# A transformer block on one core: the second norm's transposes behind every second group of pairs, and other turns for ScalarE's sums

## The chip, the cores and the metric

The kernel runs on one core of a Trainium2 chip. The metric is device time in microseconds (us); each figure is the median of several executions. Five engines work side by side, each in the order of its own instruction stream: TensorE (PE in the profile, with its weight loads as PEld), VectorE (DVE), ScalarE (ACT), GpSimd (POOL) and SyncE (SP, which only issues transfers here). They wait for each other by semaphores. TensorE writes its results into eight banks of PSUM, each 128 partitions by 512 fp32 columns; VectorE and ScalarE read them out.

## The reference

A block with an adaptive layer norm, full attention over 32 heads of 16 columns and a gated feed-forward network (FFN), for one sequence of 2048 rows and 512 columns. All is fp32, and the tolerance is such that the kernel splits operands into a high and a low part and adds three products.

```python
mod = (_silu(c) @ w_mod).reshape(c.shape[0], 6, 1, -1)
sa, ca, ga, sb, cb, gb = (mod[:, k] for k in range(6))
h = _layernorm(x) * (1 + ca) + sa
x = x + ga * attention(h, wqkv, wo)      # softmax(q k^T / 4) v, 32 heads of 16, then @ wo
h = _layernorm(x) * (1 + cb) + sb        # the second norm
x = x + gb * ((_silu(h @ w_gate) * (h @ w_up)) @ w_down)
```

## The kernel before, in words

**Units, steps and pairs.** After the projections, attention is done in 32 *units* (`NU`): four chunks of 512 query rows, and in each eight groups of four heads. A unit has 16 *steps*, one for each 128 keys, and a step has four *pairs* (`pair_of`, L977), one for each head. A pair is two matmuls, which lie in different halves of TensorE's rows and run together: the score of one head for 128 keys and 512 queries (`score`, L569), which ScalarE turns into exponentials (L571), and a score block of a unit some 20 steps ahead (`max_one`, L521), of which VectorE takes only the row maxima (L523). So each pair costs VectorE one reduction of 128x512 and ScalarE one exponential of 128x512. The variable `done` counts pairs; the first 12 come before the schedule below. There are 2048 in all, that is 512 steps.

**The second matmul.** `pv_step(i, half)` (L584) multiplies the exponentials of step `i` with V for half of the queries. It is four matmuls in four column groups of TensorE, and it adds into bank 7 over the 16 steps of a unit. There is only this one bank for it (`single`). Behind the last half of a unit ScalarE copies the bank out (L588), and `close_unit` (L924) starts what follows: transfers, a reciprocal, a product on GpSimd, and the loads for a unit three further on. `pvs` (L1012) issues the halves: never a step `i` with `4*i + 8 > done`, because its exponentials would be too fresh. In a plain group it stops behind a closed unit (`break`, L1024) and keeps what it owes for the next group; in a filler block it does not stop.

**Two kinds of stretch.** `plain(steps)` (L1041) is attention alone, in *groups* of three pairs, each followed by one or two PV halves (`HALVES` = 2, 1, 1, 2 in turn, and one more in the last group of a call). The maxima take the banks 0, 3, 1, 2 in turn, the scores 4, 5, 6. A list `tails` can put a function behind a group's pairs; it gets the next of the four banks of the maxima. `filled(places, work)` (L1056) is a *block* of eight pairs, with matmuls of a projection or of the FFN between them (`places` says how many behind which pair); they add into the banks 3 and 6, the maxima have 0, 1, 2 and the scores 4, 5. At its end come the evictions (`hook`) and then `pvs(6, False)`.

**The order by hand.** The loop at L1085 goes over the first three chunks. For each: `plain` up to the step in `STARTS` (147, 275, 403); four blocks with the output projection (`out_pair`, two for each two tiles of 128 rows); the second norm in a plain stretch; then the FFN in blocks: for each of 14 tiles of the hidden layer a `gate_up` (two blocks), for each two of them two `down` (one block each), and a `plain(WIN)` of three steps ahead of the last two. For the third chunk a `plain(REST)` stands between the norm and the FFN, and the last seven jobs are left for the end of the kernel. In `done`, chunk 0 has its projection from 588 to 620, the plain stretch from 620 to 668 and the FFN from 668 to 1016; chunk 1 the same 512 pairs later.

**The second norm.** `add_o` (L801) adds the projection to x on VectorE (L808), tile by tile, and orders ScalarE's sums: `minus_mean` (L816) and `squares` (L820), each over 128x512 with the sum of a row as a by-product. The list `behind` holds such functions with a number of *turns*; `turns_behind` counts them down at the end of each group or block and calls what has come to zero. `scaled` (L902) then forms the scale: three small steps on VectorE (L743 to L745), a chain on GpSimd (L752 to L756), four normalizations there (L765); it also orders the first load of FFN weights. `turned` (L768) is the tail: four transposes of 128x128 on TensorE into one bank (L770), ScalarE's eviction with the modulation (L772), and two operations on GpSimd (L773, L774), which leave the high and the low part for the FFN.

**The row maxima of a unit.** When all maxima of a unit are there, `after(i)` (called when `done // 4` has come to `i + 2`) hands them over, for `i + 21` = 15 mod 16. In a plain stretch it is `max_rows` (L525): a negation on ScalarE (L540), and two turns later four small matmuls into the next bank of the scores (L533 to L535), ScalarE's copy (L537) and two transfers (L539) into two rows of that unit's queries. In a filler block it is `max_turned` (L543), which has no matmul: VectorE transposes (L551, L553) and eight transfers carry the rows (L560). `beside` (L948) says which.

Of the kernel before, what the change touches and what calls it, by code (L numbers as in the profile page):

```python
# [26 lines left out]
NK = D // P  # L27
# [12 lines left out]
WIN = 3  # L40
# [3 lines left out]
PTS = 13  # L44
FBANKS = (3, 6)
KEEP = 7
REST = 24
NORM = 9
STARTS = (147, 275, 403)
TWO = (0, 3, 2, 2, 2, 2, 1, 0)  # L50
DOWN = (0, 3, 3, 0, 3, 3, 0, 0)
# [50 lines left out]
def block_kernel(ctx, tc, x, wqkv, wo, w_gate, w_up, w_down, c, w_mod, out):  # L102
# [391 lines left out]
    posts, behind = [], []  # L494
# [134 lines left out]
    def tile_mid():  # L629
        return pf.tile([P, 2, CW], F32R, name="mid", tag="mid", bufs=3)  # L630

    def tmp(name):
        return pf.tile([P, CW], F32, name=name, tag="tmp", bufs=4)
# [167 lines left out]
    def add_o(ch, t0, outs, late):  # L801
        if ch.mv is None:
            ch.mv = pf.tile([P, 4, 2], F32, name="mv2", tag="mv2", bufs=1)
            ch.rs = pf.tile([P, 4], F32, name="rs", tag="rs", bufs=1)
            ch.rs2 = pf.tile([P, 2, 4], F32, name="rs2", tag="rs2", bufs=1)
        for e in range(2):
            t = t0 + e
            nc.vector.tensor_add(ch.x2[:, t, :], outs[e], ch.x2[:, t, :])  # L808

        def sums(t):  # L810
            st = pf.tile([P, 6], F32, name="stt", tag="stt", bufs=2)
            nc.vector.bn_stats(st, ch.x2[:, t, :])
            nc.vector.bn_aggr(ch.mv[:, t, :], st)

        def minus_mean(t):
            nc.scalar.activation(tmp("sq"), ch.x2[:, t, :], AF.Identity, scale=-1.0 / D,  # L816
                                 accum_out=ch.mv[:, t, 0:1])

        def squares(t):
            nc.scalar.activation(tmp("sq"), ch.x2[:, t, :], AF.Square, bias=ch.mv[:, t, 0:1],  # L820
                                 accum_out=ch.mv[:, t, 1:2])

        if late:
            turns = (1, 2, 2, 3) if t0 == 0 else (1, 2, 3, 4)
            works = ((minus_mean, t0), (squares, t0), (minus_mean, t0 + 1), (squares, t0 + 1))
            behind.extend([k, lambda f=f, t=t: f(t)] for k, (f, t) in zip(turns, works))
        else:
            for e in range(2):
                sums(t0 + e)

    def out_pair(ch, t0, outs, halves):
        return accumulate(outs, lambda e, a, k: ch.oT[a][:, k, (t0 + e) * P:(t0 + e + 1) * P],
                          lambda b, k: ch.wo[k // 2][:, b, k % 2, :], NK,
                          lambda: posts.append(lambda: add_o(ch, t0, outs, True)), halves)
# [67 lines left out]
    def scaled(ch):  # L902
        ch.load_gu(0)
        ch.norm_scale(nc.gpsimd)
        ch.nt = [tile_mid().bitcast(F32) for _ in range(2)]
        for t in range(4):
            ch.normalize(t)
# [69 lines left out]
    def pair_of():  # L977
        nonlocal done
        i = done // 4 - 1
        most = 4 * n - 4 * (LEAD - 1)  # L980
        h = (ORDER if done < most else (0, 1, 2, 3))[done % 4]
        work = [lambda: score(i + 1, h)]
        if done < most:
            work.insert(1 - h % 2, lambda: max_one(done + 4 * (LEAD - 1)))
        for f in work:
            f()
        done += 1
        if side:
            side.pop(0)()
# [22 lines left out]
    def pvs(most, by_halves):  # L1012

        nonlocal owed
        if by_halves:
            most, owed = most + owed, 0
        while most and halves and 4 * halves[0][0] + 8 <= done:
            i, half = halves.pop(0)
            pv_step(i, half)
            most -= 1  # L1020
            if i % 16 == 15 and half:
                close_unit(i // 16, done // 4 - 1)
                if by_halves:
                    break  # L1024
        if by_halves and most and halves and 4 * halves[0][0] + 8 <= done:
            owed = most

    def turns_behind():
        for b in list(behind):
            b[0] -= 1  # L1030
            if not b[0]:
                b[1]()
                behind.remove(b)

    def end_steps():
        nonlocal ended
        while ended < done // 4:
            after(ended - 1)
            ended += 1

    def plain(steps, tails=()):  # L1041

        nonlocal four, bank, beside
        beside = False
        assert steps % WIN == 0 and done % 4 == 0
        four, bank = Turn(0, 3, 1, 2), Turn(4, 5, 6)
        for w in range(4 * steps // WIN):
            for _ in range(WIN):
                pair_of()
            if w < len(tails) and tails[w]:  # L1050
                tails[w](four())
            pvs((HALVES[(w - 2) % 4] if done > 8 else 0) + (w == 4 * steps // WIN - 1), True)
            turns_behind()
            end_steps()

    def filled(places, work):  # L1056

        nonlocal four, bank, beside
        beside = True
        four, bank = three, Turn(4, 5)  # L1060
        if done >= 4 * n - 4 * (LEAD - 1):
            places, bank = ALONE.get(places, places), Turn(4, 5, 0, 1, 2)
        for r in range(len(places)):
            pair_of()
            take(work, places[r])
            if r % 4 == 3:
                end_steps()
        hook()
        pvs(6, False)
        turns_behind()  # L1070
# [14 lines left out]
    for ci in range(last):  # L1085
        plain(STARTS[ci] - done // 4)
        ch = chunks[ci]
        for t0 in (0, 2):
            work = out_pair(ch, t0, outs, True)
            filled(TWO, work)  # L1090
            filled(TWO, work)
        behind.append([4, lambda: scaled(ch)])
        tails = [lambda tp, k=k: ch.turned(tp, k) for k in range(NK)]
        plain(NORM, [None] * NORM + tails[:3])
        plain(WIN, tails[3:])
        if ci == last - 1:
            plain(REST)
        for _ in range(len(ch.jobs) - (KEEP if ci == last - 1 else 0)):
            job, args = ch.jobs.pop(0)
            if args == (NF // FG - 1, 0):  # L1100
                plain(WIN)
            work = job(ch, *args, outs, True)
            for places in (TWO, TWO) if job is gate_up else (DOWN,):
                filled(places, work)
# [5 lines left out]
    turns = chain([2, 3, 2, 0, 1, 2, 0], cycle([1, 3, 2, 0]))  # L1110
# [19 lines left out]
    ch, chp = chunks[last], chunks[last - 1]  # L1130
# [10 lines left out]
    for t in range(4):  # L1141
        out_terms(ch, t, banks[t], (NK - 1,))
        if t % 2:
            add_o(ch, t - 1, banks[t - 1:t + 1], False)
# [40 lines left out]
```

## Time and profile before

| | |
|---|---|
| median of 3 runs | 1829.32 us (1829.18 to 1830.04) |
| span of the profiled execution, first to last instruction | 1827.6 us |
| granted TensorE clock, mean | 1.000 |
| TensorE busy | 1818.3 us (99%) |
| VectorE busy | 1523.2 us (83%) |
| ScalarE busy | 1255.7 us (69%) |
| GpSimd busy | 459.9 us (25%) |
| HBM, over the span | 144 GB/s |

The profiled execution has its span alone on record, not a time of its own like the runs; the median of the runs is 1.7 us above the span, for what lies around the first and the last instruction. Matmuls are pipelined and their ends are modelled, so TensorE shows as busy nearly all the time, also where it waits: what a stretch costs is read from the starts of its instructions, and from the gaps of VectorE. In a row of the timeline the first number is the start in us from the start of the span, the second how long the row lasts; `x6` says that six instructions of a kind are merged into it, and a bracket gives the idle time ahead of it and whose end ended it.

### The profile page before, as it was taken

What the parts mean: (1) busy time and instruction counts of PE and PEld (TensorE: products, weight loads), DVE (VectorE), ACT (ScalarE), POOL (GpSimd) and SP (SyncE); (2) the same over time, 40 slices, a digit from 0 to 9 for tenths busy, and PEclk for the clock granted to TensorE, in tenths of its full rate; (3) what the DMA queues carried; (4) which work ended last, traced back from release to release, by engine and by line L of the source; (5) the groups of instructions that cost most, each with busy time, mean ns of one, the idle gap of its engine ahead of it and who ended that gap; (6) DMA issues with size and microseconds to landing.
All of it is one profiled execution on the core that took longest, in us unless ns stands there. A gap on an engine that the chain in (4) does not pass through costs nothing.

```text
span 1827.6 us, 41072 instructions
## 1 busy us (share of the span) xinstructions
PE 1818.3 (99%) x16904; PEld 1199.7 (66%) x16904; DVE 1523.2 (83%) x2554; ACT 1255.7 (69%) x2434; POOL 459.9 (25%) x538
## 2 busy tenths in 40 slices
PE   9999999999999999999999999999999999999999
PEld 7876444444455777776565777776464577767887
DVE  5578999999999888889999888889999988821544
ACT  4223888888888776777888777777888877774211
POOL 3612544556223111111123111111113011130200
PEclk9999999999999999999999999999999999999999
DMA  9884876667845454453544554444643536333742
GB/s 306 288 225 143 202 195 178 178 167 200 206 81 125 103 123 142 114 148 71 144 110 107 139 125 119 124 115 91 160 79 57 119 89 162 130 119 120 276 167 110
DMA packets 80488, 267.63 MB, mean 146 GB/s; under 512 B 19604, under 2 KB 24212, under 8 KB 59620
## 3 DMA queue, kind: packets, MB, share of 16 engines
q1 hardware_dynamic: 61324, 179.71, 34.1%
q0 software_dynamic: 18288, 84.49, 19.4%
q8 instruction: 133, 2.18, 0.5%
q10 hardware_dynamic: 688, 0.80, 0.2%
q14 instruction: 55, 0.45, 0.1%
HBM read 201.85 MB, written 62.13 MB: 144 GB/s over the span
## 4 chain that ended last, share of the span: by engine, by line
PE 82%; DVE 14%; ACT 1%; DMA 1%; issue 0%; SPq 0%; DVEq 0%; ACTq 0%
PE bank L584 21%; PE bank L786 20%; PE bank L569 14%; DVE mx L523 14%; PE bank L521 11%; PE bank L211 7%; PE bank L796 7%; DMA wm_ab<-in_w_mod 1%; PE bank L770 0%; DMA kop<-o_dr 0%; PE bank L163 0%; DMA rb<-d_dr 0%; ACT sq L820 0%; PE bank L839 0%; DVE v_flat L870 0%
## 5 line engine op out<-in xcount | busy, mean ns | idle before, releaser
L523 DVE TENSOR_REDUCE mx<-bank 128x1 f32<-128x512 f32 x2048 | 1274.3, 686 | 108.3 <-PE bank L521 54.6
L569 PE MATMUL bank<-qop,kop 50*128 50x512 f32 x2048 | 728.6, 425 | 0.4 <-ACT pt__16523 L571 0.2
L521 PE MATMUL bank<-kop,qop 48*128 48x512 f32 x2048 | 725.1, 425 | 0.3
L569 PEld LDWEIGHTS bank<-qop,kop 50*128 50x128 f32 x2048 | 343.6, 184 | 167.9 <-issue 49.7
L521 PEld LDWEIGHTS bank<-kop,qop 48*128 48x128 f32 x2048 | 344.0, 185 | 107.0 <-DVE mx L523 62.3
L786 PE MATMUL bank<-act,wgu 64*128 64x512 f32 x1872 | 301.4, 392 | 0.0
L786 PEld LDWEIGHTS bank<-act,wgu 64*128 64x128 f32 x1872 | 197.1, 187 | 24.3
L611 POOL TENSOR_TENSOR on<-o,rb 128x512 f32<-128x512 f32 x31 | 39.8, 1285 | 506.3 <-DMA rb<-d_dr 358.9
L786 PE MATMUL bank<-wd,mid 64*128 64x512 f32 x912 | 134.1, 397 | 0.1
L858 POOL CAST mid<-m 128x512 fp32r<-128x512 f32 x40 | 24.3, 607 | 380.9 <-DVE m L856 180.2
L786 PEld LDWEIGHTS bank<-wd,mid 64*128 64x128 f32 x912 | 88.3, 186 | 15.5 <-ACT first L893 3.2
L211 PE MATMUL bank<-hT,wqs 128*128 128x512 f32 x384 | 94.4, 397 | 0.4 <-DVE wqs L351 0.4
L854 DVE SCALAR_TENSOR_TENSOR q<-th,bank 128x512 f32<-128x512 f32 x56 | 38.2, 683 | 54.3 <-ACT th L850 54.3
L211 PEld LDWEIGHTS bank<-hT,wqs 128*128 128x128 f32 x384 | 70.7, 188 | 18.8 <-issue 2.9
L850 ACT ACTIVATE th<-bank 128x512 f32<-128x512 f32 x56 | 33.3, 594 | 57.9 <-PE bank L796 57.9
L870 DVE TENSOR_TENSOR x<-bank,x 128x512 f32<-128x512 f32 x84 | 53.9, 685 | 19.0 <-PE bank L786 16.8
L856 DVE TENSOR_TENSOR m<-bank,q 128x512 f32<-128x512 f32 x56 | 38.7, 692 | 21.7 <-PE bank L796 19.7
L859 POOL TENSOR_TENSOR mid<-m,mid 128x512 fp32r<-128x512 f32 x40 | 51.6, 1289 | 3.3
L796 PE MATMUL bank<-wd,mid 128*128 128x512 f32 x216 | 51.5, 394 | 0.0
L211 PE MATMUL bank<-wqs,hT 128*128 128x512 f32 x192 | 48.1, 398 | 0.0
L786 PE MATMUL bank<-wgu,act 64*128 64x512 f32 x288 | 47.0, 393 | 0.0
L796 PEld LDWEIGHTS bank<-wd,mid 128*128 128x128 f32 x216 | 40.4, 188 | 9.0 <-POOL mid L859 0.2
(6301 smaller groups left out, 5148.9 us busy)
## 6 DMA issues: line engine op xcount, KB each, us to landing
wgu<-gu_dr SPq DMA_DIRECT2D x48, 1024.0 KB
wd<-wd_dr SPq DMA_DIRECT2D x28, 1024.0 KB
kop<-kd SPq DMA_DIRECT2D x33, 768.0 KB
kop<-kd POOLq DMA_DIRECT2D x29, 768.0 KB, 8.7
gu_dr<-wgu POOLq DMA_DIRECT2D x14, 1024.0 KB, 13.6
kd<-prt SPq DMA_DIRECT2D x16, 512.0 KB
qd<-prt SPq DMA_DIRECT2D x16, 512.0 KB
kop<-gu_dr SPq DMA_DIRECT2D x8, 1024.0 KB
```

What stands on the lines that cost most here:

```text
L211: nc.tensor.matmul(pt, lhs(a, k), rhs(b, k), start=(n == 0), stop=(n == 3 * nk - 1))
L521: nc.tensor.matmul(pm, qop[u][rows, s, qt * P:(qt + 1) * P], kop[u % 3][rows, s, kc * CW:(kc + 1) * CW], start=True, stop=True)
L523: nc.vector.tensor_reduce(mx[u][:, b, s, qt, kc:kc + 1], pm, op=ALU.max, axis=AX.X)
L569: nc.tensor.matmul(sp, kop[u % 3][rows, h // 2, kt * P:(kt + 1) * P], qop[u][rows, h // 2, :], start=True, stop=True)
L584: nc.tensor.matmul(pv[u][32 * h:32 * h + 32, cols], v_flat[:, e0:e0 + 32], p_[h][:, cols], start=(kt == 0 and half == 0), stop=(kt == 15), ...
L611: mul.tensor_mul(on, o, rb)
L786: nc.tensor.matmul(outs[e], lhs(e, a, k)[rows], rhs(b, k)[rows], start=(ph == 0 and j == 0), stop=(j == z and (ph == 1 or trade is not None)),
L796: nc.tensor.matmul(outs[e], lhs(e, a, k), rhs(b, k), start=(j == 0), stop=(j == z))
L854: nc.vector.scalar_tensor_tensor(q, th, 1.0, outs[0], op0=ALU.add, op1=ALU.mult)
L856: nc.vector.tensor_mul(m32, outs[1], q)
L859: (nc.gpsimd if slow else nc.vector).tensor_sub(mid[:, 1, :], m32, mid[:, 0, :].bitcast(F32))
L870: nc.vector.tensor_add(ch.x2[:, t, :], outs[e], ch.x2[:, t, :])
```

## The change

The plain stretch behind the output projection was a `plain(9)` of twelve groups with the first three tails behind its last three groups, and a `plain(3)` whose first group had the fourth. Now it is one `plain(15)` of twenty groups, with tails behind the groups 11, 13, 15 and 17 (counted from 0). The scale is formed two groups later (turn 6 instead of 4), and the sums of the second two tiles come in the turns 1, 3, 5 and 6 instead of 1, 2, 3 and 4. `REST` is three steps shorter, so that the third chunk has 36 steps there as before; for the chunks 0 and 1 the stretch is three steps longer, the FFN starts three steps (12 pairs) later, and the next plain stretch, up to `STARTS`, is three steps shorter.

```diff
-REST = 24
-NORM = 9
+REST = 21
+NORM = 15
+FIRST = 11
...
-            turns = (1, 2, 2, 3) if t0 == 0 else (1, 2, 3, 4)
+            turns = (1, 2, 2, 3) if t0 == 0 else (1, 3, 5, 6)
             works = ((minus_mean, t0), (squares, t0), (minus_mean, t0 + 1), (squares, t0 + 1))
...
-        behind.append([4, lambda: scaled(ch)])
+        behind.append([6, lambda: scaled(ch)])
         tails = [lambda tp, k=k: ch.turned(tp, k) for k in range(NK)]
-        plain(NORM, [None] * NORM + tails[:3])
-        plain(WIN, tails[3:])
+        plain(NORM, [tails[(w - FIRST) // 2] if w >= FIRST and (w - FIRST) % 2 == 0 else None
+                     for w in range(FIRST + 2 * NK - 1)])
```

## The prediction

> **What bounds the kernel now.** I read the page first, for its chain, and then the busy time by stage in three stretches: the norm's plain stretch and the FFN's blocks of the first chunk, and plain attention in the third.
>
> ```profile
> span 1827.6 us, 41072 instructions
> PE 82%; DVE 14%; ACT 1%; DMA 1%; issue 0%; SPq 0%; DVEq 0%; ACTq 0%
> ```
> ```profile
> core 0: us, PE busy (x) PEld busy (x) DVE busy (x) ACT busy (x) POOL busy (x), PEclk, DMA share, GB/s
> 552.80:587.90 35.10, 34.68 (x349) 17.34 (x347) 32.49 (x57) 32.37 (x68) 15.22 (x29) 1.00 0.56 117
> 594.30:866.90 272.60, 272.48 (x2884) 199.18 (x2881) 242.07 (x396) 194.93 (x372) 41.75 (x48) 1.00 0.48 117
> 1425.83:1440.17 14.34, 14.34 (x146) 6.89 (x144) 14.34 (x26) 12.38 (x25) 0.00 (x0) 1.00 0.32 49
> ```
>
> In plain attention (last row) VectorE has no gap: its reductions set the pace. In the FFN's blocks (the row before; 39 blocks and a plain of 12 pairs, so about 6.8 us a block) VectorE is idle for 30.5 us of 272.6, ScalarE for 77.7, and TensorE shows no gap: there a stop of TensorE costs its full length. In the norm's stretch VectorE is idle for 2.6 of 35.1 us. That is all that the change aims at, three times in the kernel.
>
> The timeline of plain attention gives the prices of a group. TensorE's starts:
>
> ```profile
> 1428.50 0.40 PE L584 MATMUL bank<-pt__17657,v_flat 128*32 128x256 f32 x1
> ...
> 1429.50 0.50 PE L569 MATMUL bank<-qop,kop 50*128 50x512 f32 x1
> ...
> 1430.39 0.40 PE L584 MATMUL bank<-pt__17681,v_flat 128*32 128x256 f32 x1
> ...
> 1430.96 0.50 PE L569 MATMUL bank<-qop,kop 50*128 50x512 f32 x1
> ```
> ```profile
> 1424.85 12.64 DVE L523 TENSOR_REDUCE mx<-bank 128x1 f32<-128x512 f32 x21
> ```
>
> Two PV halves take 1.00 us (1428.50 to 1429.50), three pairs 0.89, one half 0.57. VectorE needs 12.64/21 = 0.602 a pair, so 1.81 a group. A group with two halves asks 1.89 of TensorE, one with a single half 1.46: the two engines are nearly level, and TensorE makes up some 0.35 us only in a group with one half.
>
> **The tails, moved apart.** VectorE's timeline at the four tails of chunk 0, and TensorE's at the first:
>
> ```profile
> 570.93 3.67 DVE L523 TENSOR_REDUCE mx<-bank 128x1 f32<-128x512 f32 x6
> 575.05 1.89 DVE L523 TENSOR_REDUCE mx<-bank 128x1 f32<-128x512 f32 x3 [0.45 <-PE bank L521]
> 577.56 1.89 DVE L523 TENSOR_REDUCE mx<-bank 128x1 f32<-128x512 f32 x3 [0.62 <-PE bank L521]
> 580.04 3.68 DVE L523 TENSOR_REDUCE mx<-bank 128x1 f32<-128x512 f32 x6 [0.59 <-PE bank L521]
> 583.93 4.53 DVE L523 TENSOR_REDUCE mx<-bank 128x1 f32<-128x512 f32 x7 [0.21 <-PE bank L569]
> ```
> ```profile
> 572.95 0.63 PE L770 MATMUL bank<-ident,mid 128*128 128x128 f32 x4 [0.19 <-DVE mx L523]
> 573.51 0.40 PE L584 MATMUL bank<-pt__6526,v_flat 128*32 128x256 f32 x1
> ```
>
> A tail takes TensorE 0.56 us. Behind the groups 9, 10 and 11 stand two halves each (the last gets one more as the end of its call), so these groups ask 0.89 + 0.56 + 1.00 = 2.45, 0.64 over VectorE's 1.81. The first still finds 0.2 us of banked maxima (gap 0.45), the next two nothing (0.62, 0.59). The fourth has no half behind it, because PV has caught up, asks 1.45 and gives 0.36 back; three groups of two halves then lead to the gap of 0.21. Sum 1.87.
>
> After the change the call is one, its halves run on in the pattern 1, 2, 2, 1, and the tails fall on groups with 1, 2, 1 and 2 halves. Surplus over 1.81, group by group from 11: 0.21, -0.35, 0.64, 0.08, 0.21, -0.35, 0.64, 0.08, 0.08. With 0.2 banked at first and each -0.35 banked for the next, the gaps are 0.01, 0, 0.29, 0.08, 0.21, 0, 0.29, 0.08, 0.08 = 1.04. Saved: 0.8. Spreading doesn't remove the work: the two engines are too level to absorb 4 x 0.56 us. Bounds per stretch: 0 and the whole 1.87; I take 0.6, since a tail takes one of the maxima's four banks, so that less is banked than counted here.
>
> **The sums, moved.** ScalarE's sums of about 0.7 us, in the groups 0, 1 and 2, delay the exponentials, and through the three score banks TensorE. What of it reaches VectorE:
>
> ```profile
> 555.42 3.68 DVE L523 TENSOR_REDUCE mx<-bank 128x1 f32<-128x512 f32 x6 [0.33 <-PE bank L569]
> 559.02 0.21 DVE L528 TENSOR_REDUCE m<-mx 128x16 f32<-128x64 f32 x1
> 559.15 3.91 DVE L523 TENSOR_REDUCE mx<-bank 128x1 f32<-128x512 f32 x6
> ```
>
> The second six take 3.91 instead of 3.68: 0.23. The 0.33 ahead of 555.42 stands behind the last projection block and stays. I take 0.2 as saved (bounds 0 and 0.23). GpSimd's chain starts two groups later and the first tail too, so their distance stays. The FFN's first weights are ordered two groups later, on SP now behind the two transfers of L539, and stand 15 groups (15 x 1.81 = 27 us) ahead of their use. The loads that unit 9's close puts on GpSimd's queue (group 8) come behind the later normalizations; they are for unit 12. GpSimd's last tail has two groups (3.6 us) to the FFN instead of three, and the FFN takes the fourth tail's columns last. I count nothing for all these, and 1 us a stretch if that tail is late.
>
> So the aim is worth 0.8 us a stretch, 2.4 in all (bounds 0 and 3 x 2.1 = 6.3).
>
> **What the three steps do to the FFN's blocks.** PV may take step i when 4i + 8 <= done. Before, the FFN of chunk 0 starts at done = 668, so its blocks end at 676, 684, ... 708: steps up to 167, 169, ... 175. Unit 10 ends with step 175, so the fourth half of a block is the last of the unit; unit 11 begins a block later. After, it starts at 680; the blocks end at 688, ... 704, 712: steps up to 170, ... 174, 176. Now the block that ends at 712 takes step 175, closes unit 10, and goes straight on with step 176, the first of unit 11. A unit is 64 pairs, eight blocks, so this repeats for the units 10 to 14, and in chunk 1, 512 pairs on, for 18 to 22: ten times. The third chunk keeps its 36 steps.
>
> Unit 11 must not write bank 7 until ScalarE's copy (L588) has read unit 10 from it. In a block nothing stands between them: the `break` is only for plain groups. The block that ends unit 10 in the trace of before, TensorE and then ScalarE:
>
> ```profile
> 620.17 0.38 PE L584 MATMUL bank<-pt__7113,v_flat 128*32 128x256 f32 x1
> 620.37 0.38 PE L584 MATMUL bank<-pt__7141,v_flat 128*32 128x256 f32 x1
> ...
> 621.03 0.38 PE L584 MATMUL bank<-pt__7168,v_flat 128*32 128x256 f32 x1
> ```
> ```profile
> 619.63 0.59 ACT L571 ACTIVATE pt__7202<-bank 128x512 f32<-128x512 f32 x1
> 621.48 0.59 ACT L588 COPY o<-bank 128x512 f32<-128x512 f32 x1 [1.26 <-PE bank L584]
> ```
>
> Next a close in plain attention (unit 8), and who waited for L588 in the whole span:
>
> ```profile
> 524.23 0.59 ACT L588 COPY o<-bank 128x512 f32<-128x512 f32 x1
> ```
> ```profile
> 524.96 0.40 PE L584 MATMUL bank<-pt__5911,v_flat 128*32 128x256 f32 x1
> ```
> ```profile
> who waited for it (us, times):
>   PEld bank L584: 4.4, 14
> ```
>
> Inside a block the next step's PV starts at 620.37, 0.20 behind the start before it. The copy starts 0.45 after the last PV start (621.03 to 621.48) and lasts 0.59; in plain attention the next PV starts 0.14 after the copy's end (524.82 to 524.96), and the last row shows that this wait is there already, 14 times, most of it covered by a group of pairs. So in the changed block: 620.17 + 0.45 + 0.59 + 0.14 = 621.35 instead of 620.37, a stop of 0.98; with a handover of nothing 0.84, with twice 0.14 1.12. ScalarE is free then (its exponential ends at 620.22). Queued behind the stop are the rest of the block's PV and all pairs after it, so ScalarE and VectorE run dry as well, and in stretches where TensorE waits for neither. I take 0.95, a little less than the row, because the copy no longer holds up the next block's first exponential. Ten times: 9.5 us.
>
> Here a rule of the Trainium skill speaks to the size. The rows: the clock is 1.00 in all three stretches, also in the first, where TensorE's stops leave VectorE the gaps of 0.2 to 0.6 us. The page "TensorE: Matmul & The Clock Gate", section "A second HAM failure mode: psum-queue depth-cycling", says that short idles of TensorE between groups, as it cycles through PSUM banks, can make the clock fall to half and rise again. By that rule the rows should show a lower clock near such stops; this trace doesn't. It is a rival below.
>
> **Two units change their way of handing over maxima.** For the units 16 and 24 the moment (done = 1008 in chunk 0) was in the last two down blocks, so `max_turned`. Now it is in the plain three steps ahead of them: `max_rows`, whose matmuls come out two turns later, at the end of the first down block, and take bank 4 (a block's eight scores use 4 and 5 in turn, this is the ninth use). The next block begins its turns anew, so its first score takes bank 4 as well and waits for ScalarE's copy. The rows, of a plain group:
>
> ```profile
> 562.53 0.28 PE L533 MATMUL bank<-minus,m 128*16 128x128 f32 x1 [0.23 <-ACT pt__6424 L571]
> ...
> 563.07 0.49 PE L569 MATMUL bank<-qop,kop 50*128 50x512 f32 x1
> ```
> ```profile
> 563.25 0.28 ACT L537 CAST mr<-bank 48x128 fp32r<-48x128 f32 x1
> ```
>
> TensorE goes on 0.54 after L533 there, with another bank; with the same bank it goes on at the end of the copy, 563.53, so 1.0. The old way put nothing on TensorE. Two times 1.0 = 2.0 us (bounds 0.5 and 1.3 each: the matmuls alone, or a late transfer on top, as unit 16's first score is only five pairs off).
>
> **The sum** goes by the span, and the same difference holds for the median: 9.5 + 2.0 - 2.4 = +9.1, so 1836.7 for the span and 1829.32 + 9.1 = 1838.4 for the median.
>
> **The rivals.**
> (a) The stop in the blocks is hidden. For it: VectorE is 89% busy there, and if TensorE had to wait for maxima later in the block anyway, a stop before it would be free. Against: VectorE's idle time there is 30.5 us over 39 blocks, 0.78 a block, so it is VectorE that waits for TensorE. It decides when VectorE's work of a block comes to the block's 6.8 us. Then 2.0 - 2.4 = -0.4: 1828.9, no change.
> (b) As (a), and the gaps of the stretch go altogether, with the rows of (16, 24) at their low bound: 1.0 - 6.3 = -5.3: 1824.0, faster.
> (c) The clock falls at each stop: ten blocks of 6.8 us at half speed are 68 us more, 1906. Against: the clock of 1.00 beside the stops of before.
> (d) The stops are there, and the gaps of the stretch go altogether: 9.5 + 2.0 - 6.3 = +5.2: 1834.5.
>
> **How the numbers follow.** The measurement can tell about 0.2%, 3.7 us, from no change. My case has 0.83, (d) 0.07, (a) 0.06, (b) 0.02, (c) 0.02. The range of the first: stops from 0.85 to 1.05, rows of two units 1.0 to 2.6, stretch 0 to -5, so +4.5 to +13; the ends don't meet, so I take 1834.4 to 1841.5, which leaves out (a), (b), (c) and the rims. Slower by over 0.2% (above 1833.0): 0.91; same: 0.07; faster: 0.02.
>
> **What would show it.** L584 waiting for L588 goes from 4.4 us in 14 times to about 14 us, with ten waits near 0.9 in the FFN's blocks of chunks 0 and 1, eight blocks apart, each in the middle of a block's PV. L533 comes up in two more places, at the starts of the last down blocks of chunks 0 and 1, with the next score 1.0 behind it. VectorE's idle time in each norm stretch falls by less than 1 us. Chunk 2 from the norm on gains about 0.8 us and loses nothing. It is wrong if the copy in those blocks is followed at once by PV without a gap, or if the FFN's blocks take 6.8 us throughout; then the sign goes with the norm's gaps.

## The result, and the profile after

| | before | after |
|---|---|---|
| median, us | 1829.23 (1828.22 to 1830.04, 5 runs) | 1839.04 (1837.51 to 1840.13, 5 runs) |
| ratio | | 1.0055, 95% interval 1.0042 to 1.0067 |
| span of the profiled execution | 1827.6 | 1835.4 |
| mean granted clock | 1.000 | 1.000 |

The changed kernel is slower by 9.8 us; 9.1 were forecast. The two profiled spans differ by 7.8 only, because the part ahead of the first score was 1.2 us and the end 0.4 us shorter in the second one; that part is not touched. From the 589th score (index 588) to the 2041st, which holds all that the change touches, the two traces differ by 9.34 us (1139.89 against 1130.55).

In the changed kernel all lines from 49 on have moved down by one: the PV matmul is L585, ScalarE's copy of bank 7 L589, the score L570, the maxima L522 and L524, the matmuls and the copy of the row maxima L534 and L538.

First the windows of the changed kernel, with the columns that the prediction shows. The first row holds the same 39 blocks and 12 pairs of chunk 0 as the row 594.30:866.90 of before; the second is plain attention in chunk 2.

```profile
599.75:876.73 276.98, 273.45 (x2885) 197.04 (x2881) 242.08 (x396) 195.11 (x372) 41.50 (x48) 1.00 0.48 117
1433.00:1447.34 14.34, 14.34 (x148) 6.84 (x144) 14.34 (x26) 12.38 (x25) 0.00 (x0) 1.00 0.42 62
```

The stretch is 4.4 us longer with the same work (276.98 against 272.60). TensorE, which showed next to no gap there (0.12 us), now shows 3.53 us of idle time (276.98 - 273.45), and the clock stayed at 1.00. Plain attention is as it was. The idle time is five times this, here at the end of unit 10, TensorE and then ScalarE:

```profile
618.83 0.38 PE L585 MATMUL bank<-pt__7115,v_flat 128*32 128x256 f32 x1
619.91 0.40 PE L585 MATMUL bank<-pt__7134,v_flat 128*32 128x256 f32 x1 [0.71 <-ACT o L589]
```
```profile
619.28 0.58 ACT L589 COPY o<-bank 128x512 f32<-128x512 f32 x1
```

The last PV matmul of unit 10 starts at 618.83 and the first of unit 11 at 619.91, 1.08 later, where inside a block the next four PV matmuls follow at about 0.21. The bracket gives 0.71 as idle, since the end of a matmul is modelled; the starts give the loss, 0.87 a stop. There are ten such stops in the trace, five in each of the chunks 0 and 1, all of 1.08 from start to start, and the view of L589 has them in the sum of what waited for the copy (4.4 us in 14 times before):

```profile
who waited for it (us, times):
  PEld bank L585: 16.5, 25
  PE bank L585: 7.1, 10
```

The row of ten waits on PE is the ten stops, 0.71 each; the weight loads of the same halves are counted beside them, so the two rows are not to be added.

In the trace by score starts, the blocks with a stop take 7.65 to 7.84 us where most others take 6.75 to 6.9, eight blocks apart, as forecast. The forty blocks ahead of the last two take together 4.3 us more in chunk 0 and 5.0 in chunk 1.

Then the last two down blocks. TensorE and ScalarE at the end of the first of them in chunk 0:

```profile
883.79 0.27 PE L534 MATMUL bank<-minus,m 128*16 128x128 f32 x1
...
884.01 0.38 PE L536 MATMUL bank<-minus,nm 128*16 128x128 f32 x2
884.74 0.50 PE L570 MATMUL bank<-qop,kop 50*128 50x512 f32 x1 [0.35 <-ACT mr L538]
```
```profile
884.43 0.26 ACT L538 CAST mr<-bank 48x128 fp32r<-48x128 f32 x1 [1.43 <-PE bank L536]
```

The score that opens the next block waits for the copy of the bank it takes again. From the first of these matmuls (883.79) to the score (884.74) are 0.95 us. By score starts the remainder of the chunk, from this block on, is longer by 0.9 us in chunk 0 and by 0.8 in chunk 1.

Last, VectorE in the norm's stretch of chunk 0:

```profile
557.95 7.50 DVE L524 TENSOR_REDUCE mx<-bank 128x1 f32<-128x512 f32 x12
...
565.85 14.59 DVE L524 TENSOR_REDUCE mx<-bank 128x1 f32<-128x512 f32 x24
580.95 3.82 DVE L524 TENSOR_REDUCE mx<-bank 128x1 f32<-128x512 f32 x6 [0.51 <-PE bank L570]
584.94 3.68 DVE L524 TENSOR_REDUCE mx<-bank 128x1 f32<-128x512 f32 x6 [0.17 <-PE bank L570]
588.53 0.24 DVE L600 RECIPROCAL dn<-dn 128x16 f32<-128x16 f32 x1
589.16 3.82 DVE L524 TENSOR_REDUCE mx<-bank 128x1 f32<-128x512 f32 x6 [0.38 <-PE bank L522]
```

The gaps at the tails are 0.51, 0.17 and 0.38, in sum 1.06, where they were 0.45, 0.62, 0.59 and 0.21, in sum 1.87; two of the rows of six are 0.14 longer than 3.68, so they hold small waits too. The 60 pairs of the stretch take 39.0 us, against 39.5 for the 48 of before and 12 plain ones of 7.17. In chunk 2 the 36 steps from the norm on take 1.02 us less (90.28 against 91.30); the FFN's blocks behind them lose 0.28 of it, nearly all in one down block (7.19 instead of 6.91). The kernel before has a down block of 7.20 too, in chunk 0, so this may be no effect of the change.

### The profile page after: what moved, and what is told of

The parts are those of the page before. It is cut to its first block, busy times and chain, and to the rows that moved or that the text cites. A ratio compares the mean times of both kernels' runs of the same rounds, so it can differ in the third digit from the quotient of the medians.

```text
span 1835.4 us, 41091 instructions
## 1 busy us (share of the span) xinstructions
PE 1818.9 (99%) x16916; PEld 1192.6 (65%) x16916; DVE 1521.5 (83%) x2550; ACT 1255.5 (68%) x2436; POOL 458.8 (25%) x538
## 4 chain that ended last, share of the span: by engine, by line
PE 91%; DVE 6%; ACT 1%; DMA 0%; issue 0%; SPq 0%; ACTq 0%; DVEq 0%
PE bank L585 24%; PE bank L787 20%; PE bank L570 17%; PE bank L522 13%; PE bank L797 8%; PE bank L212 7%; DVE mx L524 6%; PE bank L840 1%; DMA wm_ab<-in_w_mod 0%; PE bank L771 0%; ACT o L589 0%; PE bank L164 0%; ACT th L851 0%; PE bank L536 0%; PE bank L535 0%
## 5 line engine op out<-in xcount | busy, mean ns | idle before, releaser
L524 DVE TENSOR_REDUCE mx<-bank 128x1 f32<-128x512 f32 x2048 | 1274.3, 682 | 118.6 <-PE bank L522 67.1
L570 PE MATMUL bank<-qop,kop 50*128 50x512 f32 x2048 | 728.5, 425 | 1.8 <-ACT mr L538 0.7
L522 PE MATMUL bank<-kop,qop 48*128 48x512 f32 x2048 | 722.4, 424 | 0.2
L570 PEld LDWEIGHTS bank<-qop,kop 50*128 50x128 f32 x2048 | 342.9, 184 | 172.2 <-issue 48.5
L522 PEld LDWEIGHTS bank<-kop,qop 48*128 48x128 f32 x2048 | 343.3, 184 | 107.3 <-DVE mx L524 63.0
L857 DVE TENSOR_TENSOR m<-bank,q 128x512 f32<-128x512 f32 x56 | 38.7, 691 | 21.7 <-PE bank L797 19.7
```

Source lines behind the costliest of these rows:

```text
L522: nc.tensor.matmul(pm, qop[u][rows, s, qt * P:(qt + 1) * P], kop[u % 3][rows, s, kc * CW:(kc + 1) * CW], start=True, stop=True)
L524: nc.vector.tensor_reduce(mx[u][:, b, s, qt, kc:kc + 1], pm, op=ALU.max, axis=AX.X)
L570: nc.tensor.matmul(sp, kop[u % 3][rows, h // 2, kt * P:(kt + 1) * P], qop[u][rows, h // 2, :], start=True, stop=True)
L857: nc.vector.tensor_mul(m32, outs[1], q)
```

## The experiments

Eleven kernels. The theory is that of the prediction: the three steps move the FFN's blocks against the ends of the units, and the single bank 7 then makes TensorE wait in the middle of a block. Its rivals: the moved tails or sums themselves cost the time, or the wait at bank 7 is not the copy.

**The shift alone.** Before, with three more plain steps behind the old stretch; tails and sums as they were.

```diff
-REST = 24
+REST = 21
...
-        plain(WIN, tails[3:])
+        plain(2 * WIN, tails[3:])
```

> The kernel before with one thing changed: the plain stretch behind the fourth tail is three steps longer (and REST three shorter), so that the FFN's blocks of chunks 0 and 1 start three steps later. Tails, sums and scale stay as before. Theory of the phase (the blocks now close ten units in the middle of their PV, and units 16 and 24 hand their maxima over by matmuls): ten stops of 0.9 us and two of 0.9, no gain in the norm, so about +10.5 us over before, 1839 to 1841, with ten starts of PV 1.08 us behind the last PV of a unit. Rival (the spreading of tails and sums costs the time, by GpSimd, loads or banks): as before, 1829.

1840.87 us, ratio 1.0066 (1.0054 to 1.0079). All ten stops are there; the first of them, in this kernel's trace:

```profile
620.27 0.38 PE L584 MATMUL bank<-pt__7115,v_flat 128*32 128x256 f32 x1
621.36 0.40 PE L584 MATMUL bank<-pt__7134,v_flat 128*32 128x256 f32 x1 [0.70 <-ACT o L588]
```

The same distance from start to start, to 0.01 us. The first of the last two down blocks is late too, by as much as in the changed kernel (8.01 in chunk 0, 7.66 in chunk 1). In chunk 0 the second one is late as well (7.46), by something that the changed kernel doesn't have: a score waits for the transfer of the row maxima.

```profile
889.64 0.47 PE L569 MATMUL bank<-qop,kop 50*128 50x512 f32 x1 [0.44 <-DMA qop<-mr]
```

Chunk 2, whose length is unchanged, differs by 0.01 us from before. So the whole loss, and somewhat more (11.9 us in the traces), belongs to a shift that moves neither a tail nor a sum.

**The tails without the shift.** Before, with one call of twelve steps and the tails behind the groups 9, 11, 13 and 15; sums and scale as before.

```diff
-NORM = 9
+NORM = 12
+FIRST = 9
...
-        plain(NORM, [None] * NORM + tails[:3])
-        plain(WIN, tails[3:])
+        plain(NORM, [tails[(w - FIRST) // 2] if w >= FIRST and (w - FIRST) % 2 == 0 else None
+                     for w in range(FIRST + 2 * NK - 1)])
```

> The kernel before with the spreading alone: one plain call of 12 steps, tails behind the groups 9, 11, 13 and 15, sums and scale in their old turns. The blocks keep the phase of before. Theory of the phase: no stop in the blocks, L588 is waited for as before, and the norm's stretches gain what the change gained there, 0.5 us each: -1.5 us, 1827 to 1828.5. Rival (spreading costs): at least +8 us, 1837 or more; an own danger of this kernel is the fourth tail right ahead of the FFN, which could cost up to 1 us a stretch.

1827.78 us, ratio 0.9994 (0.9985 to 1.0003): not to be told from no change. No stop is in the blocks, and the 48 pairs of the stretch take 32.26 instead of 32.36 us. By these 48 pairs the tails, spread, are worth 0.1 us a stretch. In chunk 2 plain attention goes on behind them, and there the 36 steps take 90.58 instead of 91.30 us, 0.7 less; in the chunks 0 and 1, where the FFN's blocks follow, nothing of that kind shows.

**The copy made shorter.** After, with ScalarE's copy reduced to 64 of 512 columns in the ten units.

```diff
+SHORT = (10, 11, 12, 13, 14, 18, 19, 20, 21, 22)
...
+            if u in SHORT:
+                nc.gpsimd.memset(o_[u][:, 64:CW], 1.0)
...
-            nc.scalar.copy(o_[u], pv[u])
+            w = 64 if u in SHORT else CW
+            nc.scalar.copy(o_[u][:, 0:w], pv[u][:, 0:w])
```

> The changed kernel, in which ScalarE's copy of bank 7 takes 64 of the 512 columns for the ten units that close in the middle of a block (10 to 14 and 18 to 22); the other columns are filled with ones by GpSimd when the unit begins, so for these units the attention of most queries is left out. Theory (the stop is the copy itself, end to start): the copy falls from 0.587 us to at most the 0.28 us of the 48x128 copy of the row maxima, so the gap between the PV starts in these blocks falls from 1.08 to about 0.75 us, the ten blocks take about 7.33 instead of 7.66, and the whole comes 3 to 4 us under the changed kernel, about 1835.5. Rival (the gap is a fixed cost of going from TensorE to ScalarE and back, or comes from something else that is queued there): the gap stays within 0.1 us of 1.08, and the time within 1 us of 1839.

1835.53 us, ratio to before 1.0036 (1.0022 to 1.0050). The end of unit 10, TensorE and then ScalarE (the PV matmul is L588 in this kernel, the copy L593):

```profile
620.15 0.38 PE L588 MATMUL bank<-pt__7116,v_flat 128*32 128x256 f32 x1
620.86 0.40 PE L588 MATMUL bank<-pt__7135,v_flat 128*32 128x256 f32 x1 [0.33 <-ACT o L593]
```
```profile
620.60 0.21 ACT L593 COPY o<-bank 128x64 f32<-128x64 f32 x1
```

The copy falls from 0.58 to 0.21, by 0.37, and the distance of the starts from 1.08 to 0.71, by 0.37, in all ten places; eight of the blocks with a stop fall from 7.66 to 7.29, the other two (7.84 and 7.82) as much. The kernel leaves out most columns of these ten units; its time is what is asked here. The whole is 3.5 us lower by the medians and 3.3 by the traces; ten times 0.37 would be 3.7. The copy's length goes one to one into each stop of TensorE. What stays is the way to it: the copy starts 0.45 behind the start of the last PV matmul, here as in the changed kernel, and the next starts 0.05 behind the copy's end.

**The copy made twice,** in the changed kernel and in the one before.

```diff
             nc.scalar.copy(o_[u], pv[u])
+            nc.scalar.copy(o_[u], pv[u])
```

> The changed kernel with ScalarE's copy out of bank 7 done twice in a row for each unit (the second writes the same). Theory: ten stops grow by the spacing of two ScalarE instructions of this size, 0.48 us, so by 4.8 us, and the units closed in plain stretches, where the copy is beside three pairs, add what they add in e5_twice_before. So against the changed kernel 4.8 us more than e5_twice_before against the kernel before. Rival (the stop isn't the copy): the second copy adds the same to both kernels.

> The kernel before with the copy out of bank 7 done twice. In the blocks the copy has over 4 us to the next PV, so nothing there; in the plain stretches some 17 closes have only a group of pairs beside the copy, which leaves a wait of up to 0.3 us already: up to 0.48 us each, so 0 to 8 us, 1829 to 1837, and no growth at the ten closes in the FFN's blocks.

1853.40 us (ratio 1.0130, 1.0117 to 1.0144) and 1842.37 us (1.0073, 1.0059 to 1.0087). The second copy costs about the same in both (10.9 and 10.0 us from score 588 to 2040), where the theory had 4.8 more in the changed kernel. That is what the rival expected, so this pair doesn't support the theory and doesn't tell the two apart; the assumption that it costs nothing where a unit ends with a block was wrong. Only its place differs. In the changed kernel the block with the stop grows by 0.62 (7.66 to 8.28). In the one before it is the block behind each close that grows, by 0.6 (6.84 to 7.46, 6.94 to 7.50): there the copy delays the block's first exponentials, and with two score banks TensorE soon waits (0.24 us for an exponential at 626.10, behind unit 10).

**The row maxima by the old way.** After, with the handover in the three plain steps done as in a block.

```diff
-    def plain(steps, tails=()):
+    def plain(steps, tails=(), turned=False):
...
-        beside = False
+        beside = turned
...
-                plain(WIN)
+                plain(WIN, (), True)
```

> The changed kernel with one thing undone: units 16 and 24 hand their maxima over by max_turned, as before, though they come up in the plain of three steps. Theory: the two stops at the first scores of the last down blocks go, 2 x 0.87 = 1.7 us less than the changed kernel, 1837.3, and the last down-but-one blocks of chunks 0 and 1 take 6.8 instead of 7.7 to 8.0 us. Rival (those 0.87 belong to the plain or to late weights): as the changed kernel.

1835.96 us, ratio 1.0040 (1.0028 to 1.0053). The first of the last two down blocks falls from 8.01 to 7.17 us in chunk 0 and from 7.66 to 6.82 in chunk 1, 0.84 each; the ten stops stay at 1.08. Against the changed kernel chunk 0 gains 0.8 and chunk 1 1.1 by score starts, 1.9 in all; 1.7 is the two blocks. By the ratios to before the two kernels are 2.4 us apart, which the intervals don't tell from 1.9.

**The halves held back.** After, but a block that ends a unit midway holds its last two halves until the second pair of the next block; in a second kernel also with the row maxima of the last one.

```diff
-                if by_halves:
-                    break
+                if not by_halves and halves and 4 * halves[0][0] + 8 <= done:
+                    held = 2
+                break
...
+            if r == 1 and held:
+                k, held = held, 0
+                pvs(k, False)
```

> The changed kernel, and where a block closes a unit in the middle of its PV, the last two halves (the first of the next unit) wait until behind the second pair and the first three filler steps of the next block; nothing else is moved. The copy of bank 7 then has some 1.3 us of other TensorE work beside it. Theory of the phase: the ten stops go, -8.7 to -9.1 against the changed kernel, 1829.3 to 1830.5; PV of a next unit starts with no idle time ahead of it. Rival (the 0.9 of these blocks is a price of the FFN's new place, for its loads or its bank 4, and the PV is only where it shows): the blocks stay at 7.66 and the time within 2 us of the changed kernel.

> As e8_held, and the units 16 and 24 by max_turned as in e3_turned, so that both costs of the new place are taken away and the spreading of tails and sums is left. Theory: the gains of the norm's stretches alone, 0.5 + 0.5 + 1.0 = 2.0 us less than the kernel before, 1826.5 to 1828. Rival (a cost of spreading is left): 1829 or more.

1838.57 us (1.0054, 1.0040 to 1.0067) and 1838.66 us (1.0048, 1.0035 to 1.0061): missed, by 8 us and more. The stop is gone: ten other instructions stand between the two halves now, and the block of the close takes 5.88 instead of 7.66. The next takes 8.76 instead of 6.82. Of these 1.94 us 0.87 are the moved halves themselves (6.75, a block without a close, less 5.88). A part of the rest is in the view of what the FFN's matmuls waited for, and in TensorE's row at the first place:

```profile
its engine sat idle before it (us, times) until:
  DVE m L857: 5.7, 16
```
```profile
620.47 0.43 PE L787 MATMUL bank<-act,wgu 64*128 64x512 f32 x1
621.13 0.50 PE L787 MATMUL bank<-act,wgu 64*128 64x512 f32 x2 [0.23 <-DVE m L857]
```

In the changed kernel the row of L857 has 0.3 us, once. L857 is VectorE's last step of the eviction of a gate_up: the next job's first matmuls need the bank that it reads. By the starts the wait costs 0.43 here (0.66 where 0.23 is usual). The four halves at the end of a block had covered it; two of them don't. What is left of the 1.94, about 0.6, is not assigned. So the halves can't be taken from there for nothing, and the experiment put one wait in the place of another.

**Another phase.** After, with three more steps, so that the units end with a block again.

```diff
-REST = 21
-NORM = 15
+REST = 18
+NORM = 18
```

> The changed kernel with the norm's stretch another three steps longer (18 instead of 15, REST 18), so that the blocks have the phase of before again. Theory of the phase: the ten stops are gone. Units 16 and 24 turn their maxima in a block again, but now units 11 and 19 are handed over by matmuls at the end of the first FFN block, with the same stop of 0.85: so -9.1 against the changed kernel, within 1 us of the kernel before, 1828.5 to 1830.5. Rival (spreading costs): as the changed kernel, 1838 or more.

1859.73 us, ratio 1.0170 (1.0156 to 1.0184): missed by 30 us. The ten stops are gone, as expected. Two new ones of 1.08 stand at the ends of the units 15 and 23, in the first of the last two down blocks, which takes 8.05 and 7.76; and the first block of the FFN takes 8.18 and 7.96 instead of about 7.0, for the row maxima of the units 11 and 19, as expected. The bulk is in four gate_up blocks, of 12.55, 13.83, 14.41 and 13.28 us instead of 6.75, 27 us in all. SyncE's queue and TensorE, at the first of them:

```profile
617.62 0.60 SPq L596 DMA_DIRECT2D dn<-o  x1
618.31 0.43 SPq L446 DMA_DIRECT2D kop<-kd  x1
618.83 0.38 SPq L446 DMA_DIRECT2D qop<-qd  x1
619.30 9.48 SPq L716 DMA_DIRECT2D wgu<-gu_dr  x2
```
```profile
635.19 1.16 PE L787 MATMUL bank<-act,wgu 64*128 64x512 f32 x6 [4.01 <-DMA wgu<-gu_dr]
```

Unit 10 now ends with the first gate_up (done = 708). The loads of K and Q for unit 13, on SP here and at the same time on GpSimd's queue, so go out just ahead of the 1 MB of weights for the third gate_up (619.30), whose first block starts its pairs at 630.44. In the changed kernel those weights are ordered at 607.68 for a block that starts at 620.91, and the loads of K follow at 620.58. There the weights had the DMA engines nearly to themselves, and from 612 on nothing was under way:

```profile
607.60:610.00 2.40, 2.40 (x24) 2.18 (x22) 2.36 (x5) 2.11 (x5) 1.32 (x2) 1.00 0.53 125
610.00:612.00 2.00, 2.00 (x26) 1.44 (x26) 2.00 (x4) 1.75 (x4) 0.00 (x0) 1.00 0.91 385
612.00:613.00 1.00, 1.00 (x28) 0.52 (x16) 0.31 (x1) 0.14 (x1) 0.00 (x0) 1.00 0.00 0
```

The next weights are ordered behind K loads in the changed kernel too (622.54), but their gate_up starts at 648.2, 25.7 us later, and TensorE doesn't wait. The phase of the units against the FFN's jobs has thus a second condition beside the PV bank: whether the K loads fall just ahead of a weight load that is needed soon. No kernel with the K loads alone moved was run.

**The sums alone.** Before, with the sums' turns and the scale's of the change.

```diff
-            turns = (1, 2, 2, 3) if t0 == 0 else (1, 2, 3, 4)
+            turns = (1, 2, 2, 3) if t0 == 0 else (1, 3, 5, 6)
...
-        behind.append([4, lambda: scaled(ch)])
+        behind.append([6, lambda: scaled(ch)])
```

> The kernel before, with only ScalarE's sums of the second two tiles in the turns 1, 3, 5 and 6 and the scale in turn 6; the tails stay behind the groups 9, 10, 11 and the next call's first. Theory: the sums' delay of the exponentials is some 0.2 to 0.3 us a stretch, so the three stretches take 0.6 to 0.9 us less and the whole lies at 1828.0 to 1828.8, within what can be told from no change; the first 24 pairs behind the projection take 14.9 instead of 15.17 us. Rival: with the scale formed two groups later and the first tail where it was, the first tail waits for GpSimd's normalization (6.8 us from the chain's start to its end, in before 9.4 us from the chain's start to the tail), so that one of the later tails stands still for some 0.5 to 1 us a stretch and the whole is level with before or up to 2 us over it.

1832.09 us, ratio 1.0013 (1.0004 to 1.0022): my theory missed, its rival's wait came true, with 2.7 us by the medians (2.05 by the traces) instead of up to 2. In chunk 0 the first 24 pairs take 14.88 instead of 15.18 us, 0.30 saved as expected; the next twelve take 10.56 instead of 9.45. What the tails' transposes waited for (a row that the kernel before doesn't have), and VectorE behind the first tail:

```profile
its engine sat idle before it (us, times) until:
  POOL mid L765: 6.6, 16
```
```profile
577.12 1.89 DVE L523 TENSOR_REDUCE mx<-bank 128x1 f32<-128x512 f32 x3 [1.56 <-PE bank L569]
```

GpSimd's normalizations come two groups later, the first tail does not, and VectorE's gap of 0.45 behind it becomes 1.56. The later sums pay only with later tails, as the change has both.

**Both without the shift.** Before, with twelve steps and the tails behind the groups 9, 11, 13 and 15 (the edit shown above), the second sums in the turns 1, 3, 4 and 5 and the scale in turn 5.

> The kernel before, with one plain call of twelve steps (as long as before's nine and three), tails behind the groups 9, 11, 13 and 15, the sums of the second two tiles in the turns 1, 3, 4 and 5 and the scale in turn 5: what the change wants, without the shift of three steps. Theory: nothing stops in the blocks (gaps between PV starts there 0.2 us), the stretch with sums and tails spread takes 0.3 to 0.5 us less than before's, so the whole comes 1 to 2 us under before, 1827 to 1828.2. Rival: the shift is not all that costs, and spreading the tails or sums itself brings a wait (a late tail, a late first weight of the FFN): then the whole is over before by 1 us or more.

1827.18 us, ratio 0.9987 (0.9978 to 0.9995), the only version faster than before whose interval leaves 1 out. The stretch takes 32.11, 32.12 and 32.09 us in the three chunks instead of 32.36, 32.36 and 32.35; by score starts the chunks together are 0.9 us shorter, nearly all of it in chunk 2, whose 36 steps take 90.47 instead of 91.30. The medians differ by 2.2; the 0.9 lies at the lower end of the interval (0.9 to 4.0 us), and for the 1.3 between nothing is found in the trace. The gain that the change is after is there, about a tenth of a per cent, and doesn't need the three steps.

## Why the prediction was right

**The stops in the FFN's blocks.** Forecast: ten of 0.95, +9.5. Measured: ten of 0.87 by the starts, +8.7; the blocks of both chunks take 9.3 more, and the last 0.6 lie in small pieces (the largest 0.35, in the block behind chunk 1's first stop), whose cause stays open. The place, the count and the spacing were as worked out, and the shortened copy shows that it is the copy. The term that was mis-sized is the handover back to TensorE: 0.14 was taken from plain attention, it is 0.05 here (copy's end 619.86, matmul 619.91), the same in all ten places. The 0.45 towards ScalarE and the copy itself were as in the rows.

**The two units 16 and 24.** Forecast 2.0, measured 0.84 each in the experiment that undoes it, 1.7 in all. The score follows 0.95 behind the first of the small matmuls, where 1.0 was forecast; the 0.1 that the blocks lose less than that is not assigned.

**The norm's stretch.** Forecast -0.8 each, -2.4; measured -0.5 in the chunks 0 and 1 and -1.0 in chunk 2, -2.0 in all. The split was off. The sums gave 0.3 where 0.2 was taken. The gaps at the tails did fall as counted, by 0.8, yet the tails' net share was about 0.2: part of it lies in rows of maxima that got longer, and unit 9's reciprocal (588.53) now comes within the stretch and takes VectorE's time there; the rest is not assigned. With the tails alone, in the shorter call, it was 0.1 by the 48 pairs, and 0.7 in chunk 2 over its 36 steps. So how much of it counts depends on what follows: in the FFN's blocks VectorE has idle time of its own (0.78 us a block in the kernel before), in which it can make up what it owes, while in plain attention it has none. This is an argument from the rows; no run tests it by itself. That both ends of the change (sums and tails) hang together by GpSimd was counted at nothing, rightly: the distance is kept, and none of the tails' transposes waits for GpSimd in the changed kernel.

**The sum.** 9.3 + 1.7 - 2.0 = 9.0, and 0.3 more in chunk 2's later blocks: 9.3, against 9.34 in the traces and 9.8 in the medians. That the forecast met this so closely is partly luck: the stops came 0.8 lower than forecast and the two units 0.3 lower, and the smaller gain (0.4) and 0.9 in small pieces that were not forecast made up for it.

**The rivals.** (a), (b) and (d) fall: the stops are not hidden, and the gaps don't go altogether. (c) falls: the granted clock in the stretch with five stops was 1.00. By the Trainium skill, page "TensorE: Matmul & The Clock Gate", section "A second HAM failure mode: psum-queue depth-cycling", frequent short idles of TensorE between groups can make the clock fall; five stops of 0.71 us of idle time, some 55 us apart, did not, and here the measurement decides.

## What to carry to other kernels

A single accumulator that is copied out stops TensorE for the copy and its handover where the next user of the bank follows at once (and a longer copy cost as much in another place, by way of ScalarE's exponentials), so lengthening a stretch by a few steps is to be costed by where it puts every unit's end in the blocks behind it: here three steps more cost 11 us in blocks that the edit doesn't touch (9.3 and 1.7), over five times the 2.0 that it gave where it was made. The same phase decides what the end of a unit orders ahead of a weight load, so a shift that mends one condition has to be checked against the other. And where two steps of a chain are moved (sums and tails), move them together or look at what lies between them.

## What the runs showed of the hardware

**The clock after a long stop.** In the kernel with 18 steps TensorE stands still for 4.01 us at its late weights. The windows around it, columns as above (the clock is the third number from the end):

```profile
628.00:631.00 3.00, 3.00 (x42) 1.55 (x38) 2.79 (x5) 1.76 (x5) 0.10 (x1) 1.00 1.04 224
631.00:635.00 4.00, 0.18 (x2) 0.00 (x0) 1.29 (x2) 1.05 (x2) 1.76 (x2) 1.00 0.98 188
635.00:636.00 1.00, 0.81 (x6) 0.82 (x8) 0.00 (x0) 0.00 (x0) 0.00 (x0) 0.89 1.00 360
636.00:637.00 1.00, 1.00 (x8) 0.86 (x7) 0.24 (x1) 0.20 (x1) 0.00 (x0) 0.50 0.91 385
637.00:638.00 1.00, 1.00 (x8) 0.91 (x6) 0.45 (x1) 0.40 (x1) 0.00 (x0) 0.50 0.22 90
638.00:639.00 1.00, 1.00 (x7) 0.91 (x6) 0.69 (x1) 0.60 (x1) 0.00 (x0) 0.50 0.00 0
639.00:640.00 1.00, 1.00 (x10) 0.92 (x9) 0.64 (x1) 0.60 (x1) 0.00 (x0) 0.90 0.00 0
```

The granted clock goes to 0.50, not in the stop but about half a microsecond behind its end, and is back at 1.00 some 3.3 us later. From 636.09 to 639.08 pairs of matmuls follow each other at 0.43 us instead of 0.23; seven such steps cost 1.4 us more. Of the 5.8 us that this block loses, 4.0 are the wait, and most of the rest comes with the lower clock. The Trainium skill, in the same page's section "HAM oscillation — how this bites in real kernels", gives gaps of over about 3.4 us as what makes the clock fall; the trace agrees with a fall behind 4.0 us, and with none behind 0.87.

**A load beside others.** The 1 MB of weights ordered at 619.30 held TensorE until 635.19, 15.9 us later; from 628 to 635 the DMA share is 0.98 and above, that is, the core's 16 DMA engines were all busy, with the K, Q and weight loads ordered within the same 2 us. The same load, ordered alone at 607.68 in the changed kernel, was done by 612, at most 4.3 us later: from there on its DMA share is 0.00.
